# Attention with one key head and a gated branch: two token chunks normalised on GpSimd and turned by DMA, exps on VectorE from the first key tiles, and a written-out order

## The chip, the core and the metric

One core of one Trainium2 chip runs the whole program. The metric is the device time of one execution in microseconds (us). The five engines run side by side and meet only at semaphores: TensorE (PE; its weight loads are listed as PEld), ScalarE (ACT), VectorE (DVE), GpSimd (POOL) and SyncE (SP, which here only issues transfers).

## What is computed

```python
xn = layernorm(x)                       # x: 2048 tokens x 512
q  = xn @ wq                            # 32 heads of 16
k, v = xn @ wk, xn @ wv                 # one key and one value head for all
p  = softmax(q k^T / 4)                 # per head 2048 x 2048
s  = (p v) @ wo
g  = silu(silu(xn @ w1) @ w2)           # 512 -> 1792 -> 512
out = x + s * g
```

Nearly all of the time goes into 32 x 2048 x 2048 scores: each needs a product on PE, an exponential, and a second product with the values.

## The kernel before

**Tiles.** Tokens come in 16 tiles of 128, four to a chunk (4 chunks). A score tile is 128 keys x 512 queries of one head in one PSUM bank; there are 2048 of them, in 32 groups g of 4 heads x 16 key tiles. Bank 7 (`OB`) gathers the product with the values for the group that is being closed; banks 0 to 6 are shared by score tiles and by jobs.

**Phases of PE.** PE works in two forms. An S phase (`do_S`, L1086; matmul at L946) makes 3 or 4 score tiles at once: each uses 32 rows of the array, so 4 fit side by side. When an S phase has only 3 tiles, a quarter of a job round can fill the fourth place (`piece`, L689). A C round is four matmuls of 32 columns side by side with 512 moving columns: either a PV round (`do_pv`, L1349, matmul at L1371: exps times values) or a round of a job (L577). Jobs are q (projection of queries), h (first layer of the branch), z (second layer), w (output projection). Going from one form to the other costs time on PE, so the number of S phases counts as well as the number of rounds.

**Exponentials.** An A tile gets its exp on ACT (L1845), in instructions over one, two or three neighbouring banks. A D tile gets it on DVE (`pass_d`, L1075, instruction at L1082): one instruction turns scores into the bits of a bf16 power of two, and three shifted copies (`split`, L1257) are added to it with weights 0.246, 0.207, 0.174 and 0.146 through the value matrices, which makes four PV matmuls per D tile instead of one. A shifted copy of four D tiles is one 64-bit integer add on POOL (L1291), or, seldom, one instruction on DVE (L1285). `want_d` (L959) lets D tiles begin only when the keys of all 16 tiles have been evacuated.

**Prologue.** Each chunk goes through: statistics (`bn_stats` L488, L492), 1/sqrt by integer trick and two Newton steps (L506 to L515), normalisation on DVE (`xn`, L520), 16 PE transposes into PSUM (`mk_T`, L584, L593), copies back to SBUF on DVE (L606), the K job (`mk_K`, L617, matmul L624, evacuated at L638) and the V job (`mk_V`, L647, L654, evacuated at L663). The keys for odd groups are moved 16 partitions down by a DMA that POOL issues (`add_kt1`, L1448). `xn_sb` has four slots, so a chunk is normalised only when the chunk before has been read out of its slot.

**Order.** A planner (`class Planner`, L117) keeps a clock for every engine and places one instruction after the other: `pe_step` (L1686), `act_step` (L1807) and `generic_step` (L1863) each choose what is next by rules, thresholds and seeded random picks (`SEEDS`, L22; `redraw`, L406). Durations in it are constants such as `T_P` (a DVE exp, 600 ns) and `T_P64` (a POOL shift, 1035 ns). What comes out is a fixed list per engine; on the chip each engine runs its list strictly in order and waits only for semaphores. DVE instructions that use both of its SBUF ports (`ports=2`: `xn`, the scaling of a group's output at L1431, the last sum at L808, the shifts at L1285) and POOL's shifts are never let run together: each waits for the last one of the other engine.

**Transfers.** SP issues the loads of x, wk, wv, wq, the three later chunks of x, w1, four tiles of x for the residual (`xr`, L817), w2 and wo, in that order, and then the stores (L802).

Of the kernel before, what the change touches and what calls it, by code (L numbers as in the profile page):

```python
# [20 lines left out]
J_BASE, J_END, MIXJ = 0.1, 1.0, 2  # L21
SEEDS = (  # L22
# [13 lines left out]
T_P, T_SH, T_TR, T_AF = 600.0, 600.0, 630.0, 64.3  # L36
T_P64, DV_MIN, T_LIB = 1035.0, 40, 300.0
# [15 lines left out]
PE, AC, DV, PO, SP = "PE", "ACT", "DVE", "POOL", "SP"  # L53
ENGINES = (PE, AC, DV, PO, SP)
# [42 lines left out]
class Task:  # L97
    __slots__ = ("eng", "dur", "emit", "reads", "writes", "prio", "preds", "op", "on_place", "dma", "gate", "ports", "after", "ring", "first")

    def __init__(self, eng, dur, emit, reads=(), writes=(), prio=5, preds=(), on_place=None, dma=0, gate=None, ports=1):  # L100
        self.ports, self.after, self.ring = ports, None, None
# [210 lines left out]
def bass_recurrent_scan__grouped_kv_mqa__dense_activation_silu__prompt_kernel(  # L312
# [30 lines left out]
    with ExitStack() as es:  # L343
# [97 lines left out]
        dma(SP, "w2", w2_sb[:], B_w2.rearrange("(ft p) n -> p ft n", p=P), 1792, ["w2"], prio=3)  # L441
        dma(SP, "wo", wo_sb[:], A_wo.rearrange("(o p) n -> p o n", p=P), 512, ["wo"], prio=4)
# [31 lines left out]
        xn_task, t_done = {}, set()  # L474
# [9 lines left out]
        for j in range(4):  # L484
            for t in range(4 * j, 4 * j + 4):
                if t == 1:
                    continue
                ts_ = pl.add(Task(DV, 593.0, lambda v, t=t: v.bn_stats(stats_sb[:, t, :], x_tile(t)),  # L488
                                  [xkey(t)], [("st", t)], 1 + j,
                                  gate=(lambda j=j: STG(j, xn_task, evac_kt)) if j > 1 else  # L490
                                  (lambda: ("xnT", 3) in pl.lastw) if j > 0 else None))
                pl.add(Task(DV, 66.0, lambda v, t=t: v.bn_aggr(mv_sb[:, t, :], stats_sb[:, t, :]),  # L492
                            [("st", t)], [("mv", t)], 1 + j, [ts_]))
# [3 lines left out]
        for n in first:  # L497
# [5 lines left out]
            def dv(fn, reads, writes, pre):  # L503
                return pl.add(Task(DV, 66.0, fn, reads, writes, g, [pre] if pre is not None else []))
            n0 = len(pl.tasks[DV])
            t = pl.add(Task(DV, 66.0, lambda v, a=a, b=b, w=w: v.tensor_scalar(  # L506
                w, mv_sb[:, a:b, 1], LN_EPS, None, op0=ALU.add), [("mv", i) for i in tiles], [("ve", a)], g,
# [3 lines left out]
            for it, (c0, c1) in enumerate(RSQRT_C):  # L511
# [4 lines left out]
                    out=y, in0=h, scalar=c1, in1=y, op0=ALU.add, op1=ALU.mult), [("rs", a), ("vh", a)], [("rs", a)], t)  # L516
            if g == 0:
                root_of[a] = (b, pl.tasks[DV][n0:], [aggr[i] for i in tiles])
            for i in tiles:
                xn_task[i] = pl.add(Task(DV, 323.0, lambda v, i=i: v.tensor_scalar(  # L520
                    xn_sb[:, i % 4, :], x_tile(i), mv_sb[:, i, 0:1], rstd_sb[:, i:i + 1],
                    op0=ALU.subtract, op1=ALU.mult),
                    [xkey(i), ("rs", a), ("mv", i)], [("xn", i % 4)], 1 + g, [t], ports=2,
# [89 lines left out]

        def xnT_keys(c):
            return [("xnT", t) for t in range(4 * c, 4 * c + 4)]
# [78 lines left out]
        def mk_q(oi):  # L694
            c, o = divmod(oi, NOC)

            def consume(jb, op):
                b = jb.bank
                t = Task(DV, T_P, lambda v: v.tensor_scalar(qt_sb[:, oi % NQR, :], bank(b), QSCALE, None, op0=ALU.mult),
                         [("ps", b)], [("qT", oi % NQR)], 0)  # L700
                q_done[oi] = t
# [31 lines left out]
        def gated(b, k, scale, dst, key, kind):  # L733
# [11 lines left out]
            t2.first = [t1, t2] if t0 is None else [t0]  # L745
            if t0 is not None:
# [58 lines left out]
        def final(tt, b, r=None):  # L805
# [4 lines left out]
                      [t1, xr_task[tt], out_task.get(tt - 4)], ports=2)  # L810
            fin_task[tt], out_task[tt] = t2, store(tt, t2)
# [34 lines left out]
        for c in range(1, NC):  # L846
            mk_T([4 * c, 4 * c + 1])
            mk_T([4 * c + 2, 4 * c + 3])
# [135 lines left out]

        def pick_a(n, avoid, t):
# [4 lines left out]
            for strict in (True, False):  # L990
                for gg in (g, g + 1):
                    if gg >= NG:
                        break
# [81 lines left out]
        def pass_d(b, bt, g, i, kt):  # L1075
            tot[g, i] += K

            def placed(pop):
# [5 lines left out]
                op0=ALU.mult, op1=ALU.add), [("ps", b)], [("Db", bt.b, i)], 0, on_place=placed))  # L1084

# [330 lines left out]
        def make_norm(g):  # L1416
# [18 lines left out]
            norm[("m", g)] = t3  # L1435
            if e == 1:
# [4 lines left out]
                                          gate=lambda: cc < 0 or all(tt in w_rounds for tt in range(4 * cc, 4 * cc + 4))))  # L1441

# [363 lines left out]

        def act_step():  # L1807
# [33 lines left out]
            if rx is not None and rx <= t + 25:  # L1841
                q.sort(key=lambda u: u.bank)
                b0, b1 = q[0].bank, q[-1].bank
                step = q[1].bank - b0 if n > 1 else 1
                op = pl.place(AC, 0.8333 * NQ * n + T_AF, lambda a: a.activation(  # L1845
                    pa_sb[:, s * NQ:(s + n) * NQ].rearrange("p (b n) -> p b n", n=NQ), ps3[:, b0:b1 + 1:step, :], ACT.Exp),
                    [("ps", u.bank) for u in q], [("pA", s + d) for d in range(n)])
                for d in range(n):
                    pa_busy[s + d] = 1
                st["expn"] += n  # L1850
                for k, u in enumerate(q):
                    g, i, kt = u.slot
                    pool_free.append(u.bank)
                    pvq[g][i].append((op, v_lhs(0, g, kt), pa_sb[:, (s + k) * NQ:(s + k + 1) * NQ],
                                      [("pA", s + k)] + v_reads(0, kt), ("a", s + k), None))
                return True
# [13 lines left out]

        steps = {PE: pe_step, AC: act_step, DV: lambda: generic_step(DV), PO: lambda: generic_step(PO),
                 SP: lambda: generic_step(SP)}
        idle = {e: -1.0 for e in ENGINES}
# [75 lines left out]
```

## Time and profile before

| | us |
|---|---|
| median of 2 runs (664.42 and 664.57) | 664.5 |
| span of the profiled execution, first to last instruction | 662.9 |
| around the span (start, end), by difference | 1.6 |
| PE busy in the span | 652.8 |
| ACT busy | 652.0 |
| DVE busy | 613.6 |
| POOL busy | 564.8 |

A busy PE counts the modelled length of each matmul (0.38 us), though the next round starts some 0.22 us after the one before; so stalls of PE are read from the distance between starts. A waiting engine's idle time is put down to what ended it. The granted TensorE clock is full in every slice of the span.

### The profile page before, as it was taken

Reading aid. Unit: us, or ns where it says so; the run is one execution under the profiler, and the core shown is the slowest. Engines: PE = TensorE matmul, PEld = TensorE weight load, DVE = VectorE, ACT = ScalarE, POOL = GpSimd, SP = SyncE. Lnnn points to the kernel's source line nnn. Section 1 sums busy time; section 2 is a strip of 40 time slices with the busy share of each in tenths; the row PEclk is TensorE's granted clock in tenths of the full one; section 3 lists DMA queues with packets and bytes.
Section 4 is the critical chain, followed back from the end, with each engine's and each line's share of the span. In section 5 each row is a group of like instructions: output and inputs, shape, how many; then the busy total and the mean of one; then the engine's idle time right before and its main releaser. Section 6 shows DMA issues by size and latency. Waiting matters only on the chain.

```text
span 662.9 us, 21201 instructions
## 1 busy us (share of the span) xinstructions
PE 652.8 (98%) x8958; PEld 189.3 (29%) x8959; DVE 613.6 (93%) x1085; ACT 652.0 (98%) x786; POOL 564.8 (85%) x564
## 2 busy tenths in 40 slices
PE   8899999999999999999999999999999999999997
PEld 4332222222222222222222222222222222222222
DVE  8989999999999999999999999999999999998986
ACT  7999999999999999999999999999999999999996
POOL 3059999999997889998999889899999888979973
PEclk9999999999999999999999999999999999999999
DMA  9500000000000100000000000000000001000000
GB/s 303 167 9 2 2 2 2 2 2 2 1 2 18 34 18 2 1 2 2 2 2 1 18 18 18 18 2 1 2 2 2 2 18 33 2 18 2 2 2 33
DMA packets 11501, 12.86 MB, mean 19 GB/s; under 512 B 1808, under 2 KB 10768, under 8 KB 11408
## 3 DMA queue, kind: packets, MB, share of 16 engines
q1 hardware_dynamic: 10784, 10.65, 5.0%
q8 instruction: 72, 1.18, 0.8%
q0 software_dynamic: 192, 0.46, 0.2%
q10 hardware_dynamic: 432, 0.39, 0.2%
q14 instruction: 21, 0.17, 0.1%
HBM read 8.95 MB, written 2.10 MB: 17 GB/s over the span
## 4 chain that ended last, share of the span: by engine, by line
PE 90%; ACT 4%; DVE 4%; DMA 1%; issue 0%; SPq 0%; DVEq 0%
PE ps L1371 40%; PE ps L946 30%; PE ps L577 19%; ACT pa_sb L1845 4%; DMA ds_sb<-in_A_x_dram 1%; DVE stats_sb L488 1%; DVE db_sb L1082 1%; ACT t_sb L740 0%; PE ps L593 0%; SPq L423 0%; DVE xn_sb L520 0%; DVE ds_sb L1285 0%; DVE xnT_sb L606 0%; DVE fin_sb L796 0%; DVE f_sb L1395 0%
## 5 line engine op out<-in xcount | busy, mean ns | idle before, releaser
L1845 ACT ACTIVATE pa_sb<-ps 128x1024 bf16<-128x1024 f32 (+2 forms) x689 | 615.4, 1004 | 2.9 <-PE ps L946 2.0
L1291 POOL INT64_ADD ds_sb<-db_sb x548 | 556.8, 1038 | 57.9 <-DVE otr_sb L1431 31.6
L1082 DVE TENSOR_SCALAR db_sb<-ps 128x512 uint16<-128x512 f32 x740 | 476.4, 682 | 35.5 <-PE ps L946 20.6
L1371 PE MATMUL ps<-ds_sb,v_sb 128*32 128x512 bf16 x2220 | 265.2, 384 | 0.2 <-DVE ds_sb L1285 0.2
L946 PE MATMUL ps<-qt_sb,kt_sb 32*128 32x512 bf16 x2048 | 250.3, 385 | 3.7 <-ACT pa_sb L1845 1.5
L1371 PE MATMUL ps<-pa_sb,v_sb 128*32 128x512 bf16 x1312 | 231.6, 383 | 0.2 <-DVE var_sb L512 0.2
L1371 PE MATMUL ps<-db_sb,v_sb 128*32 128x512 bf16 x740 | 161.6, 384 | 0.0
L946 PEld LDWEIGHTS ps<-qt_sb,kt_sb 32*128 32x128 bf16 x2048 | 62.7, 91 | 274.6 <-ACT pa_sb L1845 149.7
L1371 PEld LDWEIGHTS ps<-ds_sb,v_sb 128*32 128x32 bf16 x2220 | 63.8, 95 | 62.1 <-issue 45.2
L577 PE MATMUL ps<-xnT_sb,w_sb 128*32 128x512 bf16 x896 | 71.1, 383 | 0.0
L1371 PEld LDWEIGHTS ps<-pa_sb,v_sb 128*32 128x32 bf16 x1312 | 57.0, 95 | 43.3 <-issue 31.0
L577 PE MATMUL ps<-w_sb,u_sb 128*32 128x512 bf16 x776 | 62.5, 383 | 0.0
L689 PE MATMUL ps<-w_sb,u_sb 32*128 32x512 bf16 x120 | 46.2, 385 | 0.0
L1371 PEld LDWEIGHTS ps<-db_sb,v_sb 128*32 128x32 bf16 x740 | 40.0, 95 | 20.2 <-issue 15.4
L740 ACT ACTIVATE t_sb<-ps 128x512 bf16<-128x512 f32 x72 | 45.1, 626 | 0.0
L742 DVE SCALAR_TENSOR_TENSOR u_sb<-t_sb,ps 128x512 bf16<-128x512 bf16 x56 | 38.2, 683 | 1.1 <-ACT t_sb L740 0.2
L577 PEld LDWEIGHTS ps<-xnT_sb,w_sb 128*32 128x32 bf16 x896 | 18.2, 95 | 24.1 <-issue 16.1
L1427 DVE STREAM_TRANSPOSE f_sb<-ps 128x512 f32<-128x512 f32 x31 | 21.9, 706 | 1.9 <-PE ps L1371 1.8
L1448 POOL DMA_DIRECT2D kt_sb<-kt_sb x4 | 2.3, 563 | 24.9 <-DVE kt_sb L638 14.7
L577 PEld LDWEIGHTS ps<-w_sb,u_sb 128*32 128x32 bf16 x776 | 15.4, 95 | 19.9 <-issue 17.0
L577 PE MATMUL ps<-wo_sb,on_sb 128*32 128x512 bf16 x256 | 19.3, 383 | 0.0
L577 PE MATMUL ps<-xnT_sb,wq_sb 128*32 128x512 bf16 x240 | 18.7, 383 | 0.0
(83 smaller groups left out, 180.9 us busy)
## 6 DMA issues: line engine op xcount, KB each, us to landing
w_sb<-in_B_w_dram SPq DMA_DIRECT2D x2, 1792.0 KB, 14.0
xr_sb<-in_A_x_dram SPq DMA_DIRECT2D x16, 128.0 KB, 2.4
out_dram<-ob_sb SPq DMA_DIRECT2D x15, 128.0 KB, 1.7
ds_sb<-in_A_x_dram SPq DMA_DIRECT2D x3, 512.0 KB, 6.9
wq_sb<-in_A_wq_dram SPq DMA_DIRECT2D x1, 512.0 KB, 5.0
wo_sb<-in_A_wo_dram SPq DMA_DIRECT2D x1, 512.0 KB, 16.3
kt_sb<-kt_sb POOLq DMA_DIRECT2D x4, 112.0 KB, 3.8
ds_sb<-in_A_x_dram SPq DMA_DIRECT2D x2, 128.0 KB, 2.8
```

The costliest lines, as they stand in the source:

```text
L488: ts_ = pl.add(Task(DV, 593.0, lambda v, t=t: v.bn_stats(stats_sb[:, t, :], x_tile(t)), [xkey(t)], [("st", t)], 1 + j, gate=(lambda j=j: S ...
L577: last = h.matmul(bank(b)[32 * j:32 * (j + 1), 0:n], lhsT=lhs(j), rhs=rhs, start=start, stop=stop, tile_position=(0, 32 * j), skip_group_c ...
L689: return (lambda pe: pe.matmul(bank(b), lhsT=lhs(k, rows, 0, P), rhs=rhs(k, rows), start=False, stop=last, tile_position=(32 * i, 0), skip ...
L740: t1 = Task(AC, 490.0, lambda a: a.activation(t_sb[:, k, :], src, ACT.Tanh, scale=scale), [held], [("t", k)], 0, [t0])
L742: t2 = Task(DV, T_P, lambda v: v.scalar_tensor_tensor(out=dst, in0=t_sb[:, k, :], scalar=1.0, in1=src, op0=ALU.add, op1=ALU.mult), [held, ...
L946: return pe.matmul(bank(b), lhsT=kt_sb[32 * i:32 * i + 32, g % 2, kt * P:(kt + 1) * P], rhs=qt_sb[32 * i:32 * i + 32, (g // 2) % NQR, :], ...
L1082: bt.P[i] = pl.add(Task(DV, T_P, lambda v: v.tensor_scalar(db_sb[:, bt.b, i * NQ:(i + 1) * NQ], bank(b), 128.0 * LOG2E, 128.0 * (SHIFT_BET ...
L1291: whole["po"].append(pl.add(Task(PO, T_P64, lambda g, cols=cols: g.int64_add(ds_sb[:, s, cols].bitcast(U64), db_sb[:, bt.b, cols].bitcast( ...
L1371: h = pe.matmul(bank(OB)[32 * i:32 * (i + 1), cols], lhsT=lhs, rhs=rhs, start=s0, stop=s1, tile_position=(0, 32 * i), skip_group_check=True)
L1427: t1 = pl.add(Task(DV, T_TR, lambda v: v.transpose(f_sb[:, k, :], bank(OB)), [("ps", OB)], [("F", k)], 1, [norm.get(("m", g - 2))]))
L1448: kt1[c] = pl.add(Task(PO, T_SWDGE, lambda e: e.dma_start(kt_sb[DH:P, 1, cols], kt_sb[0:P - DH, 0, cols]), [("kt0", k) for k in range(4 * ...
L1845: op = pl.place(AC, 0.8333 * NQ * n + T_AF, lambda a: a.activation(pa_sb[:, s * NQ:(s + n) * NQ].rearrange("p (b n) -> p b n", n=NQ), ps3[ ...
```

## The change

1. The normalisation of tiles 8 to 15 (chunks 2 and 3) is placed on POOL instead of DVE (`XN_PO = 2`; the planner books 1200 ns for one).
2. The transposes of chunks 2 and 3 are DMA transposes within SBUF that SP issues, one per tile of 128 x 512 (`turn`), in place of 16 PE transposes and two DVE copies per chunk. The loads of w2 and wo are issued behind the last of them.
3. `want_d` asks for the keys of the first 4 tiles only (`D_TILES`). Statistics and Newton steps of later chunks get other priorities and gates. A limit `AHEAD_PA` is put on A tiles of the next group.
4. From the point at which all keys and values are evacuated (`started`), PE, ACT, DVE and POOL take their next instruction from a table, `ORDER`. A letter or a short code stands for each placement: an S phase with its banks, groups and heads and the place for a quarter round, a late score tile (`L`), a PV round with the kind of each head's operand (`P`), a new job (`N`) and a round of one (`J`), an exp over 1, 2 or 3 banks, a tanh (`T`), and so on. `order_S`, `order_pe`, `order_task` and `order_step` carry it out.
5. The planner's constants for a DVE exp and a POOL shift become 598 and 1014 ns.

In the built program this makes, before and after: D tiles 740 and 756; ACT exps over one bank 85 and 29, over two 593 and 595, over three 11 and 23; POOL shifts 548 and 567; DVE shifts 7 and 0; PE transposes 64 and 32; normalisations on DVE 16 and 8, on POOL 0 and 8; S phases that stand apart from each other 638 and 629; quarter rounds in S phases 120 and 176; matmuls on zeros that the planner puts where PE has nothing else (L577 on `zer`) 60 and 124. On POOL a library switch, which was issued once at the start for the integer add, is now issued four times more: before the normalisation of chunk 2, after it, before that of chunk 3, and after it.

```diff
+XN_PO, T_DMA, T_XN, D_TILES, AHEAD_PA = 2, 2, 1200.0, 4, 14
-T_P, T_SH, T_TR, T_AF = 600.0, 600.0, 630.0, 64.3
-T_P64, DV_MIN, T_LIB = 1035.0, 40, 300.0
+T_P, T_SH, T_TR, T_AF = 598.0, 600.0, 630.0, 64.3
+T_P64, DV_MIN, T_LIB = 1014.0, 40, 300.0
+ORDER = {
+    PE: (
+        "N1PssssS11Ah0PssssS21LZ+1PssssJS20@s2LdmJS30(MZ3N2JJJS22+9lv.PdsaaPsdssPaadsPssadPasssS21O_k.PsassPasssS22.9Gv.PsaaaPsss"
...
-        dma(SP, "w2", w2_sb[:], B_w2.rearrange("(ft p) n -> p ft n", p=P), 1792, ["w2"], prio=3)
-        dma(SP, "wo", wo_sb[:], A_wo.rearrange("(o p) n -> p o n", p=P), 512, ["wo"], prio=4)
+        for name, dst, src, kb in (("w2", w2_sb[:], B_w2.rearrange("(ft p) n -> p ft n", p=P), 1792),
+                                   ("wo", wo_sb[:], A_wo.rearrange("(o p) n -> p o n", p=P), 512)):
+            dma(SP, name, dst, src, kb, [name], prio=4).gate = lambda: T_DMA >= NC or len(turned) == 4 * (NC - T_DMA)
...
-                xn_task[i] = pl.add(Task(DV, 323.0, lambda v, i=i: v.tensor_scalar(
+                xn_task[i] = pl.add(Task(DV if g < XN_PO else PO, 323.0 if g < XN_PO else T_XN, lambda v, i=i: v.tensor_scalar(
                     xn_sb[:, i % 4, :], x_tile(i), mv_sb[:, i, 0:1], rstd_sb[:, i:i + 1],
                     op0=ALU.subtract, op1=ALU.mult),
...
+        def turn(t):
+            def placed(op):
+                t_done.add(t)
+                turned.add(t)
+            pl.add(Task(SP, 60.0, lambda e: e.dma_start_transpose(out=xnT_sb[:, :, t * P:(t + 1) * P], in_=xn_sb[:, t % 4, :]),
+                        [("xn", t % 4)], [("xnT", t)], 1, [xn_task[t]], placed, dma=128 * 1024))
...
-            mk_T([4 * c, 4 * c + 1])
-            mk_T([4 * c + 2, 4 * c + 3])
+            if c < T_DMA:
+                mk_T([4 * c, 4 * c + 1])
+                mk_T([4 * c + 2, 4 * c + 3])
+            else:
+                for t in range(4 * c, 4 * c + 4):
+                    turn(t)
...
-            if any(k not in evac_kt or evac_kt[k].op is None for k in range(NKT)):
+            if any(k not in evac_kt or evac_kt[k].op is None for k in range(D_TILES)):
...
+        def started():
+            placed = lambda ts, n: len(ts) == n and all(t.op is not None for t in ts.values())
+            return st["pro"] >= NPRO and x_free[0] and placed(evac_kt, NKT) and placed(v_task, NC) and placed(kt1, NC)
...
+        def step_of(e, own):
+            def step():
+                if ORDER and e in ORDER and ordered() and at[e] < len(ORDER[e]):
+                    return order_step(e)
+                return own()
+            return step
+
         steps = {PE: pe_step, AC: act_step, DV: lambda: generic_step(DV), PO: lambda: generic_step(PO),
                  SP: lambda: generic_step(SP)}
+        steps = {e: step_of(e, fn) for e, fn in steps.items()}
```

The order in which PE's list after the change goes through the prologue is: transposes and K and V of chunks 0 and 1, then S phases with D tiles among them, K of chunk 2, a few S phases and PV rounds, the first four matmuls of K of chunk 3, ten PV matmuls, the other twelve of K, and the sixteen of V of chunk 3. POOL's list there is: four normalisations (chunk 2), the key move of chunk 1, two shifts, four normalisations (chunk 3), the key move of chunk 2, five shifts, the key move of chunk 3, and 560 shifts.

More of the change, by code (lines that the diff above doesn't have):

```diff
@@ L503, in dv @@
             def dv(fn, reads, writes, pre):
[L504 removed]
+                return pl.add(Task(DV, 66.0, fn, reads, writes, g if g < 1 else -1, [pre] if pre is not None else []))
             n0 = len(pl.tasks[DV])
             t = pl.add(Task(DV, 66.0, lambda v, a=a, b=b, w=w: v.tensor_scalar(
[L507 removed]
+                w, mv_sb[:, a:b, 1], LN_EPS, None, op0=ALU.add), [("mv", i) for i in tiles], [("ve", a)], g if g < 1 else -1,
                 [aggr[i] for i in tiles]))
@@ L1841, in act_step @@
             if rx is not None and rx <= t + 25:
[L1842 to L1856, printed above, removed]
+                return place_exp(q, t)
             if soon is not None:
```

303 lines of the change are left out of this document (295 added, 8 removed).

## Prediction

> **What bounds the kernel now.** I read the page's first part and its chain, then busy time by windows, then groups by form, then PE's timeline.
>
> ```profile
> span 662.9 us, 21201 instructions
> PE 652.8 (98%) x8958; PEld 189.3 (29%) x8959; DVE 613.6 (93%) x1085; ACT 652.0 (98%) x786; POOL 564.8 (85%) x564
> ...
> PE 90%; ACT 4%; DVE 4%; DMA 1%; issue 0%; SPq 0%; DVEq 0%
> ```
> ```profile
> 20.00:40.00 20.00, 18.41 (x272) 7.63 (x276) 17.74 (x50) 19.39 (x33) 1.57 (x3) 1.00 0.26 81
> 100.00:200.00 100.00, 99.78 (x1372) 27.62 (x1368) 94.04 (x157) 99.84 (x121) 94.43 (x94) 1.00 0.01 2
> ```
>
> The windows' columns are PE, PEld, DVE, ACT, POOL. In the steady stretch PE and ACT are both full, DVE and POOL at 94; the chain lies 90% on PE. So a cut in PE's work is worth its length, as long as ACT is cut at least as much. Only the prologue has holes: between 20 and 40 us PE lacks 1.6 us and POOL does almost nothing.
>
> ```profile
> 304.12 0.39 PE L946 MATMUL ps<-qt_sb,kt_sb 32*128 32x512 bf16 x3
> ...
> 304.44 0.61 PE L577 MATMUL ps<-w_sb,u_sb 128*32 128x512 bf16 x8
> 304.99 0.39 PE L946 MATMUL ps<-qt_sb,kt_sb 32*128 32x512 bf16 x3
> ...
> 305.31 0.83 PE L577 MATMUL ps<-w_sb,u_sb 128*32 128x512 bf16 x12
> 306.08 0.39 PE L946 MATMUL ps<-qt_sb,kt_sb 32*128 32x512 bf16 x3
> ```
>
> From S phase to S phase PE takes 0.87 us with two C rounds between (x8) and 1.09 with three (x12). So a C round is 0.22, and an S phase with both changes of form 0.87 - 0.44 = 0.43.
>
> **The anchor.** PE runs its list in order. The last prologue job is V of chunk 3; behind it all keys and values exist and PE is never short of work. I take the time at which it ends, and the PE work that is left then.
>
> ```profile
> 34.01 1.04 PE L624 MATMUL ps<-xnT_sb,wke_sb 128*32 128x512 bf16 x16
> ...
> 35.30 0.56 PE L654 MATMUL ps<-wv_sb,xnT_sb 128*128 128x16 bf16 x16
> ```
>
> Before, V ends at 35.30 + 0.56 = 35.9. Counted in both built programs, there are left behind it 622 S phases and 1583.5 C rounds before, 609 and 1586 after: the new list has done 62 score tiles by then, not 48, and packs more (four tiles, or three and a quarter round). PE saves 13 x 0.43 - 2.5 x 0.22 = 5.0 us.
>
> **The other engines, part by part.**
>
> ```profile
> L1845 ACT ACTIVATE pa_sb<-ps 128x1024 bf16<-128x1024 f32 x593 | 562.5, 1050 | 1.3 <-PE ps L946 0.6 <-PE ps L689 0.2
> L1291 POOL INT64_ADD ds_sb<-db_sb x548 | 556.8, 1038 | 57.9 <-DVE otr_sb L1431 31.6 <-DVE ob_sb L808 13.0 <-PE ps L1371 5.5
> L1082 DVE TENSOR_SCALAR db_sb<-ps 128x512 uint16<-128x512 f32 x740 | 476.4, 682 | 35.5 <-PE ps L946 20.6 <-PE ps L689 8.5 <-POOL ds_sb L1291 1.0
> ```
>
> ACT: a pair costs 562.5/593 = 0.95, or 0.474 a tile. Sixteen tiles fewer give 16 x 0.474 = 7.6 us; that singles are joined to pairs and triples comes on top and isn't priced. It is more than PE's 5.0, so ACT doesn't bind.
>
> DVE: 16 exps more at 476.4/740 = 0.64 are 10.3; eight normalisations, four copies and seven shifts go. It has 662.9 - 613.6 = 49 us idle; nothing of this is on the path after the prologue.
>
> POOL: 19 shifts more at 556.8/548 = 1.016 are 19.3, and eight normalisations; it starts earlier (below), and can become the bound (rival B).
>
> SP: the loads of w2 and wo move behind the eight transposes, SP waiting for POOL at each; nothing but these loads and later stores is queued behind. Issued near 34 us, they cost nothing:
>
> ```profile
> w_sb<-in_B_w_dram SPq DMA_DIRECT2D x2, 1792.0 KB, 14.0
> ...
> out_dram<-ob_sb SPq DMA_DIRECT2D x15, 128.0 KB, 1.7
> ds_sb<-in_A_x_dram SPq DMA_DIRECT2D x3, 512.0 KB, 6.9
> ...
> kt_sb<-kt_sb POOLq DMA_DIRECT2D x4, 112.0 KB, 3.8
> ds_sb<-in_A_x_dram SPq DMA_DIRECT2D x2, 128.0 KB, 2.8
> ```
> ```profile
> L577 PE MATMUL ps<-w_sb,u_sb x776: 378/380/392, 100.7 to 643.8; 128*32 128x512 bf16 x194
> ```
>
> w2 lands by about 34 + 14 = 48, its first reader ran at 100.7; 50 us of other jobs cover it, and every us beyond would hold PE. PE's transposes and the two copies per chunk get no credit: PE waits there anyhow. The table, the constants and the priorities act through the order alone, which the counts hold.
>
> **When V of chunk 3 ends.**
>
> ```profile
> 19.33 0.68 DVE L638 CAST kt_sb<-ps 128x512 bf16<-128x512 f32 x1
> ...
> 21.59 1.37 DVE L520 TENSOR_SCALAR xn_sb<-ds_sb,mv_sb,rstd_sb 128x512 bf16<-128x512 bf16 x4
> 22.88 0.69 DVE L488 BATCH_NORM_STATS2 stats_sb<-ds_sb 128x6 f32<-128x512 bf16 x1
> 23.48 1.27 DVE L606 COPY xnT_sb<-ps 128x1024 bf16<-128x1024 bf16 x2
> ...
> 28.06 0.46 DVE L663 TENSOR_TENSOR v_sb<-ps,wj_sb 128x320 bf16<-128x320 f32 x1
> ```
> ```profile
> 0.78 0.74 POOL L463 MEMSET v_sb<- 128x768 bf16 x1
> 1.66 0.19 POOL L460 INT64_ADD lib_sb<-lib_sb  x1
> 1.79 2.77 POOL L463 MEMSET v_sb<- 128x768 bf16 x4
> ...
> 40.51 3.06 POOL L1291 INT64_ADD ds_sb<-db_sb  x3 [3.90 <-DVE db_sb L1082]
> ```
>
> - 1/sqrt of chunk 2 was ready at 21.6. Now DVE does three exps more ahead of it (1.9), and K's cast (0.7) and V's product (0.5) come later: 22.4.
> - A normalisation on POOL has no row. Low end: the memset, 2.77/4 = 0.69 for 768 elements, so 0.46 for 512. High end: two operations at the shift's 1.016 each, 2.0. I take 1.0, the shift's row, the nearest that reads and writes a tile. Chunk 2 is normalised at 26.4.
> - A library switch stands at L460 between two memsets, with the tiny add behind it. From the first memset's end (0.78 + 0.69 = 1.47) to the next start 1.79 they cost 0.3 together. But there the library wanted may have been the one already in place. I take 0.1 (nothing); the high end is in rival A.
> - The next two shifts need four D tiles. The fourth exp stands on DVE behind the statistics of chunk 3, a gate, K's cast and V's product. Before, the like stretch ran from 22.88 to 28.52, 5.6 us with two copies (1.2); now 5.6 - 1.2 + 0.6 = 5.0: ready at 27.4, later than POOL. Shifts to 29.5, normalisation of chunk 3 to 33.5 (1/sqrt is ready by then).
> - A DMA transpose has no row either. Transfers of 112 to 128 KB land 1.7 to 3.8 after issue; I take 2.8, the like-sized load, one following the other with POOL's tiles: 36.3.
> - PE then has K's 16 matmuls (four rounds, 0.9), ten PV matmuls (three rounds, 0.6) and V (0.56): 38.4. While PE waits, its whole list and, with it, ACT wait, so each us here is one at the end.
>
> The Trainium skill (VectorE: DVE Perf Modes, The three transpose paths) gives 1309 ns for a 128 x 128 block by DMA; no run here shows it yet. Four blocks would be an estimate of 5.2 us per tile; with the tiles overlapped the sum would be 2.4 later, in strict sequence about 15.
>
> **The sum.** V of chunk 3 is 38.4 - 35.9 = 2.5 later, 5.0 us of PE work fewer follow. Span 662.9 - 5.0 + 2.5 = 660.4, with 1.6 around it 662.0. The profiled execution's own time is so taken as the median, 664.5 (runs 664.42 and 664.57). With the low ends (0.46 and 1.7) V is 3.3 earlier: 658.7. With 2.0 a normalisation, chunk 2 ends at 30.4, 3.0 behind the exps, and chunk 3 takes 4.0 more: 669.
>
> **Rivals.**
>
> A, *the library switch is paid each time; slower.* Place: POOL's list, three switches on the way to chunk 3. Price: nothing (L460), a fetch by POOL's own queue (3.8), at most a load of 512 KB (6.9). At 3.8: 22.4 + 3.8 + 4 = 30.2, + 3.8 + 2.0 + 3.8 + 4 = 43.8, + 2.8 + 2.1 = 48.7; V ends 10.3 later than forecast: 672. At 6.9 three switches are 9.3 more: 682. It decides from about 1.2 per switch, where the gain is gone; at 5.6 the time is 2% up. For: the switch at the start shows no load, but may have found its library in place. Against: the row itself. Chance 0.22. The Trainium skill (GPSIMD Engine Reference, Instruction dispatch) says that the first call to a freshly loaded kernel costs about 6 us with no instruction to see; by that, an estimate, the time is 679. The row at L460 doesn't show it.
>
> B, *POOL becomes the bound.* Before, it needed 40.51 to 651.36 for 548 shifts:
>
> ```profile
> 645.25 6.11 POOL L1291 INT64_ADD ds_sb<-db_sb  x6 [3.34 <-DVE ds_sb L1285]
> ```
>
> Of these 610.9 us, 54 are waits, mostly for DVE's two-port operations (31.6 and 13.0). After, 560 shifts begin at about 40: 569 + 54 + 40 = 663, 11.5 us to the span's end, 1.6 around: 676. For 662 the waits must shrink to 40. For: seven shifts no longer go to DVE. Against: 0.4 us operations cost 1 us a wait, so order can shrink them. Chance 0.08.
>
> C, *transposes run one after the other:* four in sequence from 30.5 take 11.2 at 2.8 and 15.2 at 3.8, so 41.7 to 45.7 for 36.3: 667 to 671. For: one queue carries them. Against: loads of 128 KB on that queue overlap. Chance 0.12.
>
> D, *the prologue costs nothing more and PE's last waits go as well:* V as before, 659.5, less some 2 to 5 us of waits: 654 to 657. For: ACT has more room. Against: the steady stretch has 0.2 us in 100 to win. Chance 0.08.
>
> **How the numbers follow.** The forecast has 0.50, its own range 658 to 669; predicted is its middle case, 662. The range, 656 to 677, leaves out the best of D (0.05) and the upper end of A with the worst of B (0.14). A measurement can tell about 2% from no change: below 651.2 is faster (0.02, for which D would have to give 3 us more), above 677.8 slower (0.12: 0.11 for A with 5.6 or more a switch, 0.01 for B), within 0.86.
>
> **What would show it.** Right: V of chunk 3 (L782 in the new numbering) ends near 38; PE starts stay 0.87 and 1.09 apart; ACT's exps lose at least 7.6 us; POOL's waits fall to some 40. Wrong: a hole on POOL ahead of the normalisations (A); PE's S phases waiting for POOL's shifts late in the kernel (B); transposes that land more than 4 us after issue (C); or a steady stretch whose PE is no longer full, which would mean that the written order fits the chip worse than the planner's.

## The result, and the profile after

The changed kernel takes 691.34 us (two runs, 691.2 and 691.47) against 664.5: a ratio of 1.040, 95% interval 1.038 to 1.042. It is slower, by 26.8 us, and 29.3 above the 662.0 forecast. The span of its profiled execution is 689.7.

Busy time by windows of the kernel after; the columns are PE, PEld, DVE, ACT, POOL, then the granted clock of PE and DMA:

```profile
20.00:30.00 10.00, 7.64 (x120) 3.10 (x120) 9.73 (x31) 8.74 (x10) 8.31 (x5) 1.00 0.22 41
30.00:40.00 10.00, 2.43 (x28) 0.85 (x32) 0.89 (x3) 0.29 (x2) 2.71 (x3) 0.52 0.11 25
40.00:50.00 10.00, 5.69 (x68) 1.86 (x60) 6.10 (x10) 6.48 (x7) 4.62 (x3) 0.84 0.08 16
50.00:60.00 10.00, 0.00 (x0) 0.00 (x0) 0.00 (x0) 0.00 (x0) 4.34 (x3) 0.50 0.60 158
60.00:70.00 10.00, 7.36 (x81) 2.92 (x81) 3.60 (x6) 2.36 (x3) 8.01 (x9) 0.60 0.43 140
...
100.00:200.00 100.00, 99.98 (x1397) 29.51 (x1389) 92.50 (x155) 99.96 (x116) 94.56 (x94) 1.00 0.01 2
```

The steady stretch is as full as before. The loss lies between 20 and 70 us: in one slice no engine but POOL works, for 4.3 us of ten. POOL's timeline there (start, length, instruction, count, in brackets the idle time before and what ended it):

```profile
1.64 0.19 POOL L580 INT64_ADD lib_sb<-lib_sb  x1
...
21.69 8.28 POOL L641 TENSOR_SCALAR xn_sb<-ds_sb,mv_sb,rstd_sb 128x512 bf16<-128x512 bf16 x4 [9.98 <-DVE rstd_sb L635]
29.92 0.74 POOL L1589 DMA_DIRECT2D kt_sb<-kt_sb  x1
36.49 2.05 POOL L1430 INT64_ADD ds_sb<-db_sb  x2 [5.82 <-issue]
45.37 8.27 POOL L641 TENSOR_SCALAR xn_sb<-ds_sb,mv_sb,rstd_sb 128x512 bf16<-128x512 bf16 x4 [6.83 <-DVE v_sb L791]
53.59 0.74 POOL L1589 DMA_DIRECT2D kt_sb<-kt_sb  x1
61.30 5.09 POOL L1430 INT64_ADD ds_sb<-db_sb  x5 [6.96 <-issue]
```

Each time POOL goes from shifts (L1430) to normalisations (L641) or back it stands still: 5.82, 6.83 and 6.96 us. At each change between the two kinds the program has a library switch, which the trace shows as MODIFY_POOL_CONFIG rows on POOL's queue (30.9, 38.6 and 54.6 for these three). Two of the holes end in "issue", so nothing that the profile knows was awaited. The middle one is put down to DVE's product with V, but in the program the instruction behind it waits only for 1/sqrt of chunk 3, whose last step started at 29.38, and for DMA transposes of chunk 2 that had landed before: the releaser that is named is not the cause. (In the fifth experiment a hole of 6.85 at the same place is put down to an exp.) The switch before the first normalisation is free, because it falls into a wait of 9.98. A normalisation itself takes 2.07. PE, whose list holds the product of the first shift ahead of K of chunk 2, waits twice:

```profile
37.57 0.62 PE L1510 MATMUL ps<-ds_sb,v_sb 128*32 128x512 bf16 x4 [7.84 <-POOL ds_sb L1430]
...
62.38 0.62 PE L1510 MATMUL ps<-ds_sb,v_sb 128*32 128x512 bf16 x4 [15.18 <-POOL ds_sb L1430]
...
64.23 1.75 PE L752 MATMUL ps<-xnT_sb,wke_sb 128*32 128x512 bf16 x11
65.92 0.59 PE L782 MATMUL ps<-wv_sb,xnT_sb 128*128 128x16 bf16 x16
```

V of chunk 3 ends at 65.92 + 0.59 = 66.5, where I had said 38.4: 28.1 of the 29.3 us. What follows it took 627.0 before (35.9 to 662.9); in the kernel after it takes

```profile
66.50:689.70 623.20, 618.47 (x8519) 182.65 (x8518) 576.57 (x974) 612.13 (x705) 570.03 (x561) 1.00 0.03 8
```

so 3.8 less, where 5.0 was forecast. The gain is there; the start of the kernel, 30.6 later than before, ate it eight times over.

### The profile page after: what moved, and what is told of

Same layout as the page of the kernel before. It is cut to its first block, busy times and chain, and to the rows that moved or that the text cites. A ratio compares the mean times of both kernels' runs of the same rounds, so it can differ in the third digit from the quotient of the medians.

```text
span 689.7 us, 21332 instructions
## 1 busy us (share of the span) xinstructions
PE 654.9 (95%) x9039; PEld 199.0 (29%) x9039; DVE 611.2 (89%) x1082; ACT 642.9 (93%) x746; POOL 601.5 (87%) x591
## 4 chain that ended last, share of the span: by engine, by line
PE 45%; ACT 44%; POOL 4%; DVE 4%; issue 2%; POOLq 0%; DVEq 0%
ACT pa_sb L1957 42%; PE ps L1510 20%; PE ps L1081 14%; PE ps L698 9%; ACT t_sb L869 2%; POOL xn_sb L641 2%; POOL ds_sb L1430 2%; DVE db_sb L1220 1%; PE ps L1894 1%; DVE stats_sb L608 1%; PE ps L752 0%; DVE xnT_sb L727 0%; DVE kt_sb L766 0%; POOL kt_sb L1589 0%; PE ps L817 0%
## 5 line engine op out<-in xcount | busy, mean ns | idle before, releaser
L1957 ACT ACTIVATE pa_sb<-ps 128x1024 bf16<-128x1024 f32 (+2 forms) x647 | 606.4, 1059 | 34.2 <-PE ps L1081 33.7
L1430 POOL INT64_ADD ds_sb<-db_sb x567 | 576.4, 1038 | 53.3 <-DVE otr_sb L1570 22.0
L1220 DVE TENSOR_SCALAR db_sb<-ps 128x512 uint16<-128x512 f32 x756 | 483.7, 682 | 43.3 <-PE ps L1081 28.5
L1510 PE MATMUL ps<-ds_sb,v_sb 128*32 128x512 bf16 x2268 | 295.4, 385 | 23.0 <-POOL ds_sb L1430 23.0
L1510 PE MATMUL ps<-pa_sb,v_sb 128*32 128x512 bf16 x1296 | 251.0, 384 | 0.6 <-DVE v_sb L791 0.6
L1510 PE MATMUL ps<-db_sb,v_sb 128*32 128x512 bf16 x756 | 192.2, 385 | 1.2 <-DVE db_sb L1220 1.1
L1510 PEld LDWEIGHTS ps<-ds_sb,v_sb 128*32 128x32 bf16 x2268 | 73.1, 95 | 92.0 <-issue 47.6
L1510 PEld LDWEIGHTS ps<-pa_sb,v_sb 128*32 128x32 bf16 x1296 | 61.4, 95 | 40.4 <-issue 28.1
L698 PE MATMUL ps<-xnT_sb,w_sb 128*32 128x512 bf16 x852 | 64.7, 382 | 0.0
L1510 PEld LDWEIGHTS ps<-db_sb,v_sb 128*32 128x32 bf16 x756 | 47.4, 95 | 27.2 <-issue 15.9
L641 POOL TENSOR_SCALAR xn_sb<-ds_sb,mv_sb,rstd_sb 128x512 bf16<-128x512 bf16 x8 | 16.5, 2074 | 16.8 <-DVE rstd_sb L635 10.0
```

The lines of the kernel that those rows point to most:

```text
L641: xn_task[i] = pl.add(Task(DV if g < XN_PO else PO, 323.0 if g < XN_PO else T_XN, lambda v, i=i: v.tensor_scalar(xn_sb[:, i % 4, :], x_til ...
L698: last = h.matmul(bank(b)[32 * j:32 * (j + 1), 0:n], lhsT=lhs(j), rhs=rhs, start=start, stop=stop, tile_position=(0, 32 * j), skip_group_c ...
L1220: bt.P[i] = pl.add(Task(DV, T_P, lambda v: v.tensor_scalar(db_sb[:, bt.b, i * NQ:(i + 1) * NQ], bank(b), 128.0 * LOG2E, 128.0 * (SHIFT_BET ...
L1430: whole["po"].append(pl.add(Task(PO, T_P64, lambda g, cols=cols: g.int64_add(ds_sb[:, s, cols].bitcast(U64), db_sb[:, bt.b, cols].bitcast( ...
L1510: h = pe.matmul(bank(OB)[32 * i:32 * (i + 1), cols], lhsT=lhs, rhs=rhs, start=s0, stop=s1, tile_position=(0, 32 * i), skip_group_check=True)
```

## The experiments

My theory after the result: POOL pays some 6 us for each switch of its library and twice my price for each normalisation, and PE, running its list in order, carries both to the end. Rivals: the profile's holes are an artefact and the length alone did it; the DMA transposes are late; the order table costs. In all experiments but the eighth the instruction lists are those of the kernel after, with only the named instructions moved, added, altered or taken out; in the cuts `put(op, e, after)` moves an instruction on engine `e` behind another, and `more` adds one. Times are set against the kernel before on the same chip, 664.5 to 664.7 throughout. The second to fifth experiments are one execution each; five of the first took 667.8 to 669.2.

### 1. Normalisations back on VectorE

```diff
+for c in (2, 3):
+    at_dv = rs_task[c].op
+    for t in range(4 * c, 4 * c + 4):
+        at_dv = put(xn_task[t].op, DV, at_dv)
```

> The changed kernel with one thing undone: the eight normalisations of chunks 2 and 3 run on VectorE again, chunk by chunk right behind their 1/sqrt; transposes by DMA, early exps and the order table stay, and so does the order of every other instruction on every engine. GpSimd then has no hole of 5.8, 6.8 or 7.0 us and no 16.5 us of normalising ahead of chunk 3. Theory (GpSimd's change between the two kinds of work, with the 2.07 us of each normalisation, set the end of the prologue): TensorE gets the first shift at about 30 instead of 37.6 and goes through the 8.7 to 9.6 us of work up to the next waited-for shift without the wait of 15.2; V of chunk 3 ends near 42 (range 38 to 44) instead of 66.5, and the time is 691.3 - 24.5, about 667 (663 to 669). Rival 1 (the DMA transposes or the queue in front of w2 are what is late): V of chunk 3 stays behind 55 and the time above 680. Rival 2 (the order table itself costs): V of chunk 3 near 42, but 630 or more from there to the end instead of 623.2, so 673 or more.

Measured: 668.66, ratio to before 1.006 (1.0047 to 1.0074). POOL's timeline of this kernel has no switch left; the holes that remain are waits for VectorE:

```profile
29.18 2.08 POOL L1430 INT64_ADD ds_sb<-db_sb  x2 [1.41 <-DVE var_sb L634]
36.27 0.54 POOL L1589 DMA_DIRECT2D kt_sb<-kt_sb  x1 [5.01 <-DVE kt_sb L766]
36.85 5.08 POOL L1430 INT64_ADD ds_sb<-db_sb  x5
```
```profile
43.70:666.30 622.60, 617.76 (x8517) 182.59 (x8518) 576.44 (x974) 612.01 (x705) 569.83 (x561) 1.00 0.03 9
```

V of chunk 3 ends at 43.7, and 622.6 follow. So 22.7 us of the loss lie in POOL's part (less what the normalisations now cost on VectorE), and neither the transposes nor the table bring it: both rivals fall. But the kernel is still not faster than before.

### 2 and 3. Switches without length, length without switches

Second: the same instruction on 16 elements stays on POOL at each place, the real work goes to VectorE. Third: fills of about the same length, around which the trace has neither a switch nor a hole.

```diff
+at_po = more(PO, lambda g, t=t: g.tensor_scalar(
+    ob_sb[:, 0, 16 * t:16 * t + 16], x_tile(t)[:, 0:16], mv_sb[:, t, 0:1], rstd_sb[:, t:t + 1],
+    op0=ALU.subtract, op1=ALU.mult), op.deps, at_po)
```
```diff
+for k in range(3):
+    at_po = more(PO, lambda g: g.memset(
+        ob_sb[:].rearrange("p a d -> p (a d)")[:, 0:716], 0.0), (op.deps if k < 1 else []) + prev, at_po)
+    prev = [at_po]
```

> The kernel of the first experiment (normalisations on VectorE) with, at the place of each of the eight on GpSimd, the same instruction on 16 elements a partition into a buffer that is not in use yet: the changes of kind stay, the time of the work goes. It adds work that the result does not use. Theory (each change costs 5.8 to 7.0 us of GpSimd): two of them follow each other between the second and the third shift, 31 to about 45.6; the third shift ends at 46.7, V of chunk 3 near 50, and the time is near 675 (670 to 679), so 8 above the first experiment. Rival (the length of the normalisations did it, the holes are an artefact of the profile): within 2 us of the first experiment.

> The counterpart: normalisations on VectorE, and at the place of each of the eight on GpSimd three fills of 716 elements a partition (about 0.69 each, by the row of the fills of 768 elements at 0.737), 2.07 us together, waiting for what the normalisation waited for; GpSimd stays with one kind of work. It adds work that the result does not use. Theory: no hole of 6 us or more; first shift at about 31, eight fills' worth to 41, third shift ends near 43, V of chunk 3 near 46, time near 671 (667 to 674), some 20 below the changed kernel. Rival (the length of the normalisations did it): within 5 us of the changed kernel, above 686.

Measured: 680.79 and 673.95. The second lies above my range: I had let its first switch begin at 22.9, but the copy of keys in front of it waits for a cast on DVE until 27.0, and so all three switches lie open:

```profile
27.02 0.74 POOL L1589 DMA_DIRECT2D kt_sb<-kt_sb  x1 [3.44 <-DVE var_sb L626]
33.62 2.05 POOL L1430 INT64_ADD ds_sb<-db_sb  x2 [5.85 <-DVE db_sb L1220]
42.67 1.68 POOL L2231 TENSOR_SCALAR ob_sb<-ds_sb,mv_sb,rstd_sb 128x16 bf16<-128x16 bf16 x4 [7.00 <-DVE db_sb L1220]
44.29 0.74 POOL L1589 DMA_DIRECT2D kt_sb<-kt_sb  x1
50.92 5.10 POOL L1430 INT64_ADD ds_sb<-db_sb  x5 [5.88 <-issue]
```

The 16-element instructions take 0.43 each (median), the holes 5.85, 7.00 and 5.88. In the third kernel there is no hole before a shift:

```profile
21.56 9.07 POOL L2232 MEMSET ob_sb<- 128x716 bf16 x12 [10.06 <-DVE rstd_sb L635]
30.58 0.53 POOL L1589 DMA_DIRECT2D kt_sb<-kt_sb  x1
31.15 2.06 POOL L1430 INT64_ADD ds_sb<-db_sb  x2
```

Against the first experiment the switches alone cost 12.1 us, the length alone 5.3, both together (the kernel after) 22.7. They don't add, in part because one uses up the slack that hides the other: in the first experiment PE took up the third shift only at 40.9, while it was ready at 37.9. From the third kernel to the one after, the switches are worth 17.4 us: three of 5.8 to 7.0, less some slack. The two kernels differ a little in more than that: four normalisations' worth of fills takes 9.07, the normalisations 8.28, and the third kernel has the normalisations on VectorE as well.

### 4. One switch on the path instead of three

```diff
+po = pl.order[PO]
+last = xn_task[15].op
+early = po[po.index(xn_task[11].op) + 1:po.index(xn_task[12].op)]
+for op in early:
+    last = put(op, PO, last)
```

> The changed kernel with the first two shifts of GpSimd (and the copy of keys in front of them) moved behind the normalisations of chunk 3: all eight normalisations stay on GpSimd at 2.07 us each, but GpSimd changes its kind of work once on the path instead of three times. Theory: normalisations of both chunks end near 39, one hole of about 6, first shift ends near 47 instead of 37.5, third near 49 instead of 62.4; TensorE's 9 us of work between them now comes behind the first shift, so V of chunk 3 ends near 60 (57 to 61) and the time is near 685 (681 to 687). Rival (the changes are free and the holes mean something else): the first shift is 8 us later than in the changed kernel and nothing is won, 691 to 700.

Measured: 686.0. All normalisations run in one go, then one hole, then shifts only:

```profile
21.70 16.50 POOL L641 TENSOR_SCALAR xn_sb<-ds_sb,mv_sb,rstd_sb 128x512 bf16<-128x512 bf16 x8 [10.03 <-DVE rstd_sb L635]
38.15 0.74 POOL L1589 DMA_DIRECT2D kt_sb<-kt_sb  x1
45.18 2.05 POOL L1430 INT64_ADD ds_sb<-db_sb  x2 [6.29 <-issue]
```

The first shift is 8.7 later than in the kernel after, and the whole 5.3 earlier, as the theory had it; V of chunk 3 ended at 61.4, just past the theory's 57 to 61.

### 5. Another pair of operations

```diff
-                    xn_sb[:, i % 4, :], x_tile(i), mv_sb[:, i, 0:1], rstd_sb[:, i:i + 1],
-                    op0=ALU.subtract, op1=ALU.mult),
+                    xn_sb[:, i % 4, :], x_tile(i), *((mv_sb[:, i, 0:1], rstd_sb[:, i:i + 1]) if i < 8 else (rstd_sb[:, i:i + 1], mv_sb[:, i, 0:1])),
+                    op0=ALU.subtract if i < 8 else ALU.mult, op1=ALU.mult if i < 8 else ALU.add),
```

> The changed kernel with another pair of operations in GpSimd's eight normalisations: times 1/sqrt, plus mean, instead of minus mean, times 1/sqrt. It changes the computation for the tokens of chunks 2 and 3 (the mean is added to the scaled token); everything else, the waits too, stays. If the pair of operations is what makes one take 2.07, they come down to 1.0 or less (VectorE's takes 0.41 for the same tile): 4 us fewer ahead of the first shift, as many ahead of the third, V of chunk 3 near 58 and the time near 683 (681 to 685). If the engine takes 2.07 for 512 elements whatever the pair, nothing moves: 691 (689 to 693). The 16-element ones of the second experiment took about 0.46 each, so the length does count; I take the second, 0.6 to 0.4. The holes of 5.8 to 7.0 stay in both.

Measured: 681.07. I had bet on the other outcome: the pair does matter, 2072 ns against 763, by the rows of L641 on POOL of this kernel and, from its page, of the one after:

```profile
L641 POOL TENSOR_SCALAR xn_sb<-ds_sb,rstd_sb,mv_sb x8: 758/763/772, 22.3 to 44.1; 128x512 bf16<-128x512 bf16 x8
```
```profile
L641 POOL TENSOR_SCALAR xn_sb<-ds_sb,mv_sb,rstd_sb 128x512 bf16<-128x512 bf16 x8 | 16.5, 2074 | 16.8 <-DVE rstd_sb L635 10.0
```

Eight times 1.31 is 10.5; the time fell by 10.3. So with the switches on the path nearly every us of normalising arrives at the end. My 1.0 would have been above the price of the better pair. The Trainium skill (GPSIMD Engine Reference, Elementwise — side-by-side cycle accounting) gives 769 ns for 512 elements as this engine's best case; this row agrees for (mult, add), and the other pair is far from it.

### 6. No normalisation at all

```diff
+gone = {id(xn_task[t].op): rs_task[t // 4].op for t in range(8, 16)}
+for q in pl.order.values():
+    q[:] = [o for o in q if id(o) not in gone]
...
```

> The changed kernel with the eight normalisations of chunks 2 and 3 left out on every engine; the DMA transposes wait for the 1/sqrt of their chunk and copy what the buffer holds (tokens of chunk 1), so keys, values and hidden units of those chunks are made from other tokens. It bounds the change from below: what it would give if GpSimd did its part in no time. The first experiment left 5.2 us between my forecast for the end of V of chunk 3 (38.4) and what it measured (43.65). Theory a (VectorE's 2.8 us of normalising did that, by a wait of 1.4 on TensorE at 24.9 and the lower clock behind it, matmuls of 0.61 instead of 0.39 up to 32.4): V of chunk 3 ends at 38.5 to 40.3 and the time is 661 to 665. Theory b (my path to V of chunk 3 left out TensorE's own work and its waits for VectorE's exps between the chunks): V of chunk 3 ends at 41 or later even so, and the time is 665.5 or more; the change could then not win by whatever engine normalises.

Measured: 665.09, ratio 1.001 (1.000 to 1.002), between the ranges of the two theories. With these lists no engine that normalises could have made the change win. In the profiled execution V of chunk 3 ended at 42.7, as theory b has it, but part of that is a fall of the clock (experiments 10 and 11).

### 7. One trip in the steady stretch

```diff
+po = pl.order[PO]
+more(PO, lambda g: g.tensor_scalar(
+    lib_sb[:, 0:2].bitcast(BF16), wj_sb[:, 0:2], mv_sb[:, 0, 0:1], rstd_sb[:, 0:1],
+    op0=ALU.subtract, op1=ALU.mult), [], po[len(po) // 2])
```

> The first experiment's kernel (normalisations on VectorE) with a single instruction of GpSimd's other kind put between two shifts in the middle of the steady stretch: 2 elements a partition, into a buffer nobody reads any more, no wait of its own. It prices one trip of GpSimd out and back where nothing else is changed. The trace should show two holes of 5.8 to 7.0 around it, 13 us together with the instruction. GpSimd is 91 to 95% busy there, so the shifts have little lead: theory, most of it reaches TensorE, 668.7 + 9 = 678 (672 to 682). Rival (the eight buffers of shifted exps cover it): 668 to 670. Rival (the holes in the prologue were waits and not changes of kind): no holes, 668.7.

Measured: 681.81, ratio to before 1.026 (1.0246 to 1.0277). POOL around the place, the one long wait of PE behind it, and the window:

```profile
327.01 12.23 POOL L1430 INT64_ADD ds_sb<-db_sb  x12 [0.56 <-DVE otr_sb L1570]
346.60 0.39 POOL L2230 TENSOR_SCALAR lib_sb<-wj_sb,mv_sb,rstd_sb 128x2 bf16<-128x2 f32 x1 [7.36 <-issue]
352.78 8.13 POOL L1430 INT64_ADD ds_sb<-db_sb  x8 [5.79 <-issue]
```
```profile
353.87 0.61 PE L1510 MATMUL ps<-ds_sb,v_sb 128*32 128x512 bf16 x1 [11.17 <-POOL ds_sb L1430]
```
```profile
300.00:400.00 100.00, 88.15 (x1188) 25.00 (x1185) 82.62 (x141) 87.07 (x99) 82.08 (x83) 0.95 0.02 5
```

The holes are 7.36 and 5.79 around an instruction of 0.39 that waits for nothing: 13.5 us on POOL, 13.1 at the end. PE waits 11.2 us for the shift, so the buffers hide some 2 of the 13.5; but behind the wait PE works at a clock of 0.50 for 3.0 us (353.9 to 356.9), which takes some of that back. This is the cleanest price of a switch here: 7.4 us out and 5.8 back.

### 8. Without the table

```diff
-XN_PO, T_DMA, T_XN, D_TILES, AHEAD_PA = 2, 2, 1200.0, 4, 14
+XN_PO, T_DMA, T_XN, D_TILES, AHEAD_PA = 4, 2, 1200.0, 4, 14
-ORDER = {
...
+ORDER = {}
```

> The changed kernel without the order table and with the normalisations on VectorE by the planner, so the steady stretch is ordered by the planner as before; DMA transposes and early exps stay. It prices the table: from the end of V of chunk 3 to the end it took 622.65 in the first experiment and 627.0 in the kernel before. If the table gives the 4 us, this one takes 626 to 628 from there and, with V of chunk 3 at 40 to 44, 668 to 673 in all. If early exps and DMA transposes (less work of TensorE and more done ahead) give them, it takes 622 to 624 from there and 664 to 669 in all.

Measured: 687.5, far outside both ranges. V of chunk 3 ended at 50.7, and behind it

```profile
50.70:685.30 634.60, 626.96 (x8506) 178.05 (x8507) 583.24 (x982) 616.62 (x729) 566.34 (x557) 0.99 0.03 10
```

PE is busy for 627.0 here and 617.8 in the first experiment. So early exps and DMA transposes alone, ordered by the planner, don't bring the gain; for this start the planner's rules give an order 12 us worse than the table's and 7.6 worse than what they gave the kernel before. A part of both differences is the clock, which stood at 0.50 here from 50.7 to 56.1 (by an estimate some 2 us, as a round takes 0.40 there and 0.22 at the full clock). The table is worth 12 us against the one and 4 against the other. Its worth by itself on the old start stays open: it can only be replayed on its own start.

### 9. Normalisations later on VectorE

```diff
-for c in (2, 3):
-    at_dv = rs_task[c].op
+for c, at_dv in ((2, v_task[1].op), (3, rs_task[3].op)):
```

> The first experiment's kernel with the four normalisations of chunk 2 put further down VectorE's order: behind the casts of chunk 1's keys and values instead of in front of the statistics of chunk 3. In the first experiment TensorE waited 1.4 for VectorE's hidden-unit product at 24.9, and the matmuls behind it took 0.61 instead of 0.39 from 26.3 to 32.4. Theory a (the wait brought the lower clock): no wait of 1.4 there, matmuls near 0.39 from 24 to 32, V of chunk 3 ends at 40 to 42.5 instead of 43.65, and the time is 665 to 667.5. Theory b (VectorE is short of time in 21 to 33 wherever its 2.8 us of normalising stand): the wait comes back at the exps behind it, V of chunk 3 ends at 43 to 45 and the time is 668 to 670. Neither beats 664.6: the sixth experiment left the normalisations out altogether and took 665.1.

Measured: 672.06, ratio to before 1.011 (1.0095 to 1.0129): worse than either theory. The wait came back as 1.4 for an exp and 1.4 for the transposes of chunk 2, and the clock stayed down longer:

```profile
20.00:30.00 10.00, 7.45 (x121) 3.14 (x125) 9.79 (x31) 7.91 (x10) 2.56 (x3) 0.97 0.19 39
30.00:40.00 10.00, 8.06 (x76) 2.50 (x68) 6.47 (x14) 3.44 (x5) 2.16 (x4) 0.50 0.51 114
40.00:50.00 10.00, 9.11 (x101) 2.73 (x97) 5.70 (x10) 5.51 (x7) 5.43 (x7) 0.68 0.72 226
```

V of chunk 3 ended at 47.6. At neither of the two places were VectorE's 2.8 us free: against the sixth experiment they cost 3.6 us at the first and 7.0 at the second, the lower clock included.

### 10 and 11. More and fewer rounds on zeros

```diff
+for n, at_pe in ((7, fills[-4]), (6, fills[-1])):
+    for k in range(n):
+        at_pe = more(PE, at_pe.emit, [], at_pe)
```
```diff
+pe[:] = [o for o in pe if o not in fills or o.deps[1:]]
```

(`fills` are the rounds on zeros.)

> The sixth experiment's kernel (normalisations of chunks 2 and 3 left out, their tokens copied from chunk 1) with 13 more of the rounds on zeros that the planner puts where TensorE has nothing else: 7 (0.76 us) in front of the wait of 0.76 at 27.67, 6 behind the round at 29.7. They do no useful work. In the sixth experiment TensorE was busy for 9.77 of the 12 us from 24 to 36 (11.15 before), and then ran at a granted clock of 0.52 from 36 to 43, matmuls of 0.61 to 0.64 instead of 0.39: 6.5 x (1 - 0.39/0.63) = 2.5 us, of the 3.1 us that it stood above my forecast. Theory a (the clock follows how busy TensorE was): the clock from 36 to 43 stays above 0.9, V of chunk 3 ends near 41 (0.6 of added rounds, 2.5 saved), the time is 662 to 664. Theory b (the clock falls there for another cause): 0.5 to 0.6 again, and the time is 665 to 666.5.

> The sixth experiment's kernel with 10 of its 14 rounds on zeros between 24 and 30 us taken out (they do no useful work). Theory a (the clock follows how busy TensorE was): the granted clock falls sooner than at 35.7, so more matmuls take 0.6; V of chunk 3 ends at 44 to 46 and the time is 666 to 669. Theory b (another cause): the fall stays at about 35, V of chunk 3 ends at 41.5 to 42.7, the time is 664 to 665.

Measured: 665.38 and 665.53, so no difference from the sixth (665.09). The windows of the sixth kernel's profiled execution and of the eleventh's:

```profile
24.00:36.00 12.00, 9.77 (x146) 4.13 (x149) 11.27 (x26) 8.92 (x10) 5.36 (x7) 0.99 0.46 97
36.00:43.00 7.00, 6.48 (x66) 1.97 (x59) 2.45 (x5) 2.54 (x3) 2.82 (x3) 0.52 0.95 313
```
```profile
24.00:36.00 12.00, 9.09 (x112) 3.15 (x112) 11.31 (x27) 9.58 (x11) 5.74 (x7) 1.00 0.46 97
36.00:43.00 7.00, 6.23 (x90) 2.22 (x90) 4.52 (x8) 4.23 (x6) 4.70 (x6) 1.00 0.99 326
```

With more rounds the clock held in the profiled execution and V of chunk 3 ended at 40.6, as theory a says, but the median time is b's. With fewer, PE was busy for less (9.09 of 12) and the clock held all the same, so theory a is wrong as I had put it; b forecast a fall at 35 and a time of 664 to 665, and is wrong too. The fall differs from run to run: the ten runs of the sixth kernel took 664.0 to 665.6 seven times and 666.7 to 667.2 three times, and its profiled execution, at 667.2, was one of the latter; the eleventh's took 664.7. The tenth had three such runs in ten, the eleventh five, the kernel before none. So the fall costs about 2 us when it comes; what decides whether it comes wasn't settled (the last section has what the traces show). Without it V of chunk 3 ends at 40.2 in the eleventh kernel, not at 42.7.

## Why the prediction was wrong

The last matmul of V of chunk 3 orders nearly all the runs: the time of the profiled execution less the moment at which it ended is 624.4 to 625.0 for the kernel after and all experiments but the seventh, whose trip stands behind it (638.1), and the eighth, without the table (636.5). So the anchor was the right one, and what follows it was forecast well: 622.0 of span, measured 622.6 to 623.2. What failed is the working of *when V of chunk 3 ends*, in this order of size:

- **"A library switch ... I take 0.1 (nothing)."** It is 5.8 to 7.0, three times on the path: 17.4 us by the third experiment against the kernel after. The row at L460 was the wrong witness: in the kernel after the same first add stands at 1.64 without a hole, and the three switches on the path are paid. I had said myself that the library wanted may have been in place, and still took the row's value; why that first one is free no run shows. Rival A named the mechanism and the three places, and that came true. That its 6.9 is near the holes is luck: it was the time of a 512 KB load, and no load is seen at a switch (from 340 to 355 us in the seventh experiment the DMA's share is 0.00). Its 682 is still 9 short, for the next reason.
- **"A normalisation on POOL ... I take 1.0."** It is 2.07, the high end of my bounds: 8 x 1.07 = 8.6, and the fifth experiment shows that such us arrive nearly in full.
- **The way to V.** I let K and V start when the transposes land, with PE ready. Without any normalisation V ends at 40.2 (eleventh kernel) and not 38.4, 0.6 more follow, and with the falls of the clock in some runs the time of the sixth is 665.1: 3.1 over the forecast. What my path lacked is PE's own list. In the eleventh kernel's profile it goes from the product of the first shift to that of the third in 8.6 us, and from there to V's end in 2.7:

```profile
28.91 0.59 PE L1510 MATMUL ps<-ds_sb,v_sb 128*32 128x512 bf16 x4
...
37.48 0.40 PE L1510 MATMUL ps<-ds_sb,v_sb 128*32 128x512 bf16 x4
...
39.65 0.56 PE L782 MATMUL ps<-wv_sb,xnT_sb 128*128 128x16 bf16 x16
```

My first shift was ready at 28.4 (27.4 and one shift of 1.0); 28.4 + 8.6 + 2.7 is 39.7, so most of the 1.8. This is worked out from the profile; no run shortens that list. Of the 8.6, 1.9 are short waits for DVE.

17.4 + 8.6 + 3.1 is 29.1 of the 29.3. The terms come from different kernels (see the third experiment), so that they close so well is partly luck. Rival A's formula comes near too: 660.9 + 3 x 6.5, plus 8.6, is 689.0.

Why the range (to 677) missed too: both unknown prices were bounded by themselves, 6.9 and 2.0, but their high ends were never added. They would have given 660.9 + 20.7 + 8 x 1.0 = 690. The Trainium skill (GPSIMD Engine Reference, Instruction dispatch) had about 6 us for the first call to a freshly loaded kernel; the traces agree (5.8 to 7.4), and each return costs about as much.

Right were: the fourth exp (forecast 27.4, its row at 26.74 plus 0.68), that POOL starts on 1/sqrt (at 21.7; forecast 22.4), the cover of w2's load (issued at 54.9, first read at 133.2), and the transposes (forecast 2.8 after issue):

```profile
xnT_sb<-xn_sb SPq DMA_TRANSPOSE x8, 2.5
```

So rival C falls: in the first experiment SP issued the four of a chunk 1.3 apart, so they overlap. The Trainium skill's 1309 ns for a 128 x 128 block (VectorE: DVE Perf Modes, The three transpose paths) would be 5.2 for a tile of four, an estimate; a tile landed 2.5 after its issue. B falls as well: in the first experiment 560 shifts behind the prologue fit into 622.6 us beside a full PE. The saving behind V came to 3.8 to 4.4 where 5.0 was forecast.

Even with both prices at nothing the change would not have won: V of chunk 3 ends 4.3 us later than before (40.2 for 35.9, eleventh kernel), and what follows is 4.3 shorter. No version here beats the kernel before.

## What to carry to other kernels

Before moving an instruction to GpSimd, write down which library it needs and count the changes in that engine's list: each costs 5.8 to 7.4 us in this kernel, on the way out and on the way back, even for two elements. A wait of 9.98 us hid one; the buffers of the steady stretch hid some 2 of 13.5 us. If work of both kinds must run there, put all of one kind together (the fourth experiment won 5.3 us so), and choose the pair of operations by its measured time. And where two prices have no row for the same reason, add up their high ends before giving a range.

## What the runs showed of the hardware

- GpSimd's normalisation of 128 x 512 bf16 takes 2.07 us as (subtract, mult) and 0.76 as (mult, add); VectorE's takes 0.41. On 16 elements a partition GpSimd's takes 0.43.
- An instruction named MODIFY_POOL_CONFIG on GpSimd's queue, 1 to 42 ns long, is all that the profile records of a switch; the hole behind it is put down to "issue" or to an unrelated producer. Behind the start such rows stand in the kernel after and in the second, fourth, fifth and seventh experiments, and in the first, third, sixth and eighth there are none. From shifts to the other kind the hole was 6.8 to 7.4 us, back 5.8 to 7.0.
- The granted clock was 1.00 or 0.50, and the stretches at 0.50 that ended within a run lasted a multiple of 3.41 us: 6.83 in the first and sixth experiments, 17.07 in the ninth, 10.24 and 20.48 in the kernel after. In these three experiments it fell behind single waits of 1.4 us or less: in the 3.41 us before the fall TensorE was busy for 47% (first), 54% (ninth) and 70% (sixth), while 69% in the eleventh brought no fall. In the ninth it stayed at 0.50 with TensorE 84% busy. The Trainium skill (TensorE: Matmul & The Clock Gate, What's actually happening) has the clock fall after an idle window of some 3.4 us and come back after a busy one of that length. The length agrees, and so does that the moment differs from run to run; but here the clock fell with TensorE busy for up to 70% of such a stretch, and was slower to come back.

The sixth kernel before and in its stretch at 0.50, and the eleventh's stretch without a fall, in the columns of the windows above:

```profile
32.44:35.85 3.41, 2.38 (x35) 0.99 (x38) 2.91 (x6) 2.91 (x4) 2.65 (x4) 1.00 0.62 136
35.85:42.68 6.83, 6.56 (x62) 1.89 (x55) 2.28 (x4) 2.69 (x3) 2.97 (x3) 0.50 0.93 305
```
```profile
34.38:37.79 3.41, 2.35 (x31) 0.71 (x31) 2.42 (x5) 2.99 (x4) 3.41 (x5) 1.00 0.57 164
```
